# VectorE's and ScalarE's order in the first 21 steps taken from a list schedule that the program works out while it is made

## Chip, cores and metric

The kernel runs on one core of a Trainium2 chip. The metric is the time of one execution on the device in microseconds (us). Before the change the median of three runs is 1159.02 us (1157.17 to 1159.98). The engines are TensorE (PE in the rows: matrix products; PEld is its loading of weights), VectorE (DVE), ScalarE (ACT), GpSimd (POOL) and SyncE (SP, which here issues the DMA transfers). Each engine works through its own instructions in the order in which the program was written. "Granted clock" is the share of full speed that TensorE was given; it has two levels, 2.4 GHz (1.0) and 1.2 GHz (0.5).

## What is computed

A decaying linear attention (32 heads, 768 tokens, width 64) gives 3072 tokens of width 512. Two feed-forward layers follow, each 512 to 2048 to 512, the first with a leaky ReLU between its products, the second with an ELU. The weights come in as float64.

```python
def _moe_ref(x, w_in, w_out):
    h = x @ w_in
    g = np.maximum(0.01 * h, h)
    return (g @ w_out).astype(np.float32)

def _moe2_ref(x, w_in, w_out):
    h = x @ w_in
    g = np.where(h > 0.0, h, np.exp(np.minimum(h, 0.0)) - 1.0)
    return (g @ w_out).astype(np.float32)

x = attention(q, k, v)            # 4 x 8 x 768 x 64 -> 3072 x 512
return _moe2_ref(_moe_ref(x, w_in1, w_out1), w_in2, w_out2)
```

## The kernel before

**Tiling.** The tokens are cut into 6 blocks of 512 (`j`), the hidden width of 2048 into 16 slices of 128 (`m`). One *step* is one slice for one block: a first product (`gemm1`, L254: 12 matmuls of 128x512 into `h`), the leaky ReLU on ScalarE (`leaky`, L343, tile `gf`), a split of the result into a high and a low part (high: a cast on ScalarE, tile `ghi`; low: a subtraction on VectorE, tile `glo`; for steps 4 to 7 both lie in a waiting tile, `gx`), and a second product (`gemm2`, L273: 12 matmuls that add up in two accumulators `y0` and `y1`). Every product is made of three matmuls, high by high, high by low and low by high, so that a result near float32 comes out.

**Weights.** The float64 weights of a slice are turned into a high and a low float32 part on the chip. This *conversion* is done piece by piece. A piece is half a slice for slices 0 to 3 (8 pieces: the half of the first product and that of the second) and a whole slice for slices 4 to 15 (12 pieces). Its operations are `c_put` (ScalarE, L113), `c_exp` (VectorE, two instructions, L116 and L117), a bias (ScalarE, L120), `c_top` (VectorE, L123), `c_low` (VectorE, L127), `c_sign` (VectorE, L131), `c_mul` (VectorE, L134, with a cast on ScalarE, L172) and `c_split` (VectorE, L176). `conv_ops` (L182) puts them into one queue, and `conv(n)` (L198) takes n of the VectorE operations from its front.

**Order of the first layer.** The first layer's steps are numbered by visits: steps 0 to 3 are block 0 with slices 0 to 3, steps 4 to 11 block 1 with slices 0 to 7, steps 12 to 23 block 0 with slices 4 to 15, steps 24 to 31 block 1 with slices 8 to 15. Then come blocks 2 to 5 with all 16. A table `plan` (L505, L506) says in which order the first products run (0, 4, 1, 5, 2, 6, 3, 7, 8, 9, ...), up to which step the second products have to be done behind each (`drain`, L299), and how many operations of the conversion are put in at two places of each step (`conv(n1)` between the first product and its leaky ReLU, `conv(n2)` at the step's end). `need` (L211) forces the conversion of a piece that a product is about to read. When the last slice of a part visit is done (steps 3 and 11), `drain` copies the accumulators out (tile `ysb`, two copies on VectorE, two on ScalarE, L320) and SP writes them to HBM; the next block's second product can't begin before that.

**Around it.** Before the first step, the eight attention chunks of blocks 0 and 1 run. Chunk 8 and later are worked between the steps from step 23 on; the loads of chunks 8 and 9 are issued at steps 8 and 9. The weights of slices 6 to 15 are loaded by `load_w` at the ends of steps, into tiles that other data (chunks, waiting tiles, `ysb`) held before. The order on VectorE, ScalarE and SP is that in which this loop is written.

Of the kernel before, what the change touches and what calls it, by code (L numbers as in the profile page):

```python
# [20 lines left out]
F32 = mybir.dt.float32  # L21
F32R = mybir.dt.float32r
# [5 lines left out]
ALU = mybir.AluOpType  # L28
# [4 lines left out]
P = 128  # L33
# [5 lines left out]
BLK = 512  # L39
CPB = BLK // C  # L40
NB = NT // BLK
KD = DM // P
MF = DFF // P
HM = MF // 2
V0 = 4
# [9 lines left out]
def body(ctx: ExitStack, tc: tile.TileContext, kkv, w1, w2, tabs, out):  # L55
    nc = tc.nc
    big = ctx.enter_context(tc.tile_pool(name="big", bufs=1))
    wp = ctx.enter_context(tc.tile_pool(name="wp", bufs=1))
    cv = ctx.enter_context(tc.tile_pool(name="cv", bufs=2))
    gp = ctx.enter_context(tc.tile_pool(name="gp", bufs=2))  # L60
    ps = ctx.enter_context(tc.tile_pool(name="ps", bufs=1, space=PSUM))
# [3 lines left out]
    pscr = [dp.tile([P, KD, BLK], F32, name=f"pscr{j}") for j in range(2)]  # L65
# [6 lines left out]


    W = 2 * BLK
    raw, wt, cvt, exps, ready = {}, {}, {}, [], {}
    nload = nload2 = 0


# [1 line left out]
    pieces = [(m, a, 1) for m, a in halves] + [(m, 0, 2) for m in range(V0, MF)]  # L80
    loaded = set()
# [37 lines left out]
    def bias(e):  # L119
        nc.scalar.activation(e.bitcast(I16), e, AF.Relu, bias=ebias, scale=2.0**3)  # L120
# [22 lines left out]
    def c_exp(i):  # L143
        e = cvt[i][0]
        s = cv.tile([P, i[2] * BLK], U16, tag="s", name="s", bufs=1)
        cvt[i].append(s)
        masks(e, s)
        exps.append(e)

    def c_top(i):  # L150
        m, a, n = i
# [10 lines left out]
    def c_mul(i):  # L162
        e, _, f = cvt.pop(i)
        power(e, f)
        m, a, n = i
        t = place(m, a, n, F32R, "w")
        for k in range(n):
            wt[0, m, a + k] = t[:, k * W : (k + 1) * W]
        t = t.rearrange("p (a b c) -> p a b c", a=n, b=2)
        f = f.rearrange("p (a c) -> p a c", a=n)  # L170
        ready[i] = t, f
        nc.scalar.copy(t[:, :, 0, :], f)  # L172

    def c_split(i):
# [7 lines left out]
    def conv_ops():  # L182
        yield c_put, pieces[0]
        for n, i in enumerate(pieces):
            yield c_exp, i
            if n:
# [6 lines left out]
            yield c_mul, i  # L193
        yield c_split, pieces[-1]

    queue = list(conv_ops())

    def conv(n):  # L198

        while queue and queue[0][1][:2] in loaded:  # L200
            op, i = queue[0]
            if op is not c_put:
                if not n:
                    break
                n -= 1
            queue.pop(0)
            op(i)
            while exps:
                bias(exps.pop(0))

    def need(m, a):  # L211
        while (m, a) not in split_done:
            conv(1)
# [129 lines left out]
    def leaky(h):  # L343
        gf = gp.tile([P, BLK], F32, tag="gf", name="gf", bufs=2)
        nc.scalar.activation(gf, h, AF.Prelu, alpha=0.01)  # L345
        return gf


    with ExitStack() as actx:
        ab = actx.enter_context(tc.tile_pool(name="ab", bufs=1))  # L350
        ap_ = actx.enter_context(tc.tile_pool(name="ap", bufs=2))
        aps = actx.enter_context(tc.tile_pool(name="aps", bufs=1, space=PSUM))
# [102 lines left out]
        nload = V0  # L455
# [20 lines left out]
        o = outputs(0, *next(banks))  # L476
# [6 lines left out]
        for c in range(1, 2 * CPB):  # L483
# [3 lines left out]
            o = outputs(c, *next(banks))  # L487
# [20 lines left out]
        for n, (s, upto, n1, n2) in enumerate(plan):  # L508
# [11 lines left out]
            if 4 <= s < 8:  # L520
                i = 2 * (s % 2)
                ghi, glo = g[s] = [wait[s // 2 - 2][:, i + k, :] for k in range(2)]
                nc.scalar.copy(ghi, gf)
                nc.vector.tensor_tensor(glo, gf, ghi.bitcast(F32), ALU.subtract)
            else:
                split_g(s, gf, nc.vector, gp, 3)
            drain(upto, stage_w if vi < 2 or m < m0 + 2 and vi == 2 else stage_f)
            c = sc_at.get(s)
            if c is not None:
                sc = scores(c, aps, "x")  # L530
                prep(c)
                masked(c, sc, ap_, "pt")
            conv(n2)
            if s in (8, 9):
                att_load(2 * CPB + s - 8)
            if nload < (MF - 1 if s > 11 else MF - 3) or vi > 1 and m > m0 + 1:
                load_w()
            if vi > 3:

                if m == 2 and npre < 2 * MF:  # L540
                    pre_load()
                if 2 < m < MF - 1:
                    pre(m < MF - 2)
            if m0 > 0 and m == m1 - 3:
                need(MF - 1, 1)
                reload(0, j, stage_f)


    with ExitStack() as ectx:
# [44 lines left out]
        for s in range(NA, 2 * NS):  # L594
            ph, j, m, (_, _, m0, m1, vi) = steps[s]
            if s % 4 == 0:
                h = ps.tile([P, BLK], F32, tag="h", name="h")
# [3 lines left out]
            if ph == 0:  # L601
                gf = leaky(h)
# [80 lines left out]
```

## Time and profile before

| | us |
|---|---|
| median of three runs | 1159.02 (1157.17 to 1159.98) |
| the profiled execution, its own time | 1159.4 |
| its span, from the first to the last instruction | 1157.6 |
| TensorE busy | 1138.3 |
| VectorE busy | 653.2 |
| ScalarE busy | 542.2 |
| mean granted clock of TensorE | 0.995 |

The 1.8 us between the profiled execution's time and its span lie outside the instructions. All times inside the trace count from the start of the span. A row of a timeline gives the start, the length and the operation, and in brackets how long the engine was idle before it and who ended the wait. A busy TensorE isn't TensorE at its full clock, so the granted clock is read beside the busy time.

### The profile page before, as it was taken

The page shows a single profiled execution, that of the slowest core. Times are in us where ns is not written, and L with a number is a line of the kernel's source. Part 1 is how long each engine was busy: PE and PEld are TensorE (multiplying, and loading weights), DVE is VectorE, ACT ScalarE, POOL GpSimd, SP SyncE. Part 2 cuts the span into 40 slices and gives each one's busy share as a digit, 9 for nine tenths or more (in the row PEclk, how much of TensorE's full clock was granted, in tenths as well). Part 3 has the DMA queues.
Part 4 walks back from the last instruction along what each step waited for, and adds up shares of the span by engine and source line. Part 5 has one row for each costly group of instructions (what it writes and reads, how often), then busy time and mean ns, then how long its engine had stood idle before and what let it go on. Part 6 is the DMA issues. An engine that isn't in the chain of part 4 may idle for free.

```text
span 1157.6 us, 14906 instructions
## 1 busy us (share of the span) xinstructions
PE 1138.3 (98%) x6024; PEld 930.9 (80%) x6024; DVE 653.2 (56%) x1049; ACT 542.2 (47%) x901; POOL 93.2 (8%) x77
## 2 busy tenths in 40 slices
PE   8989999999999999999999999999999999999998
PEld 6767788788888888888888888888888888888886
DVE  5879773235654564651212666666666666766655
ACT  2555552224444443441323654654654655555553
POOL 4000001102221222220000000000000000000000
PEclk9989999999999999999999999999999999999999
DMA  9931303334554554430645400100100100000000
GB/s 377 377 129 54 109 21 116 115 115 154 193 200 154 193 195 151 161 131 1 218 183 196 148 19 1 55 19 1 55 19 1 55 19 1 37 1 1 37 1 37
DMA packets 29877, 117.10 MB, mean 101 GB/s; under 512 B 3312, under 2 KB 3312, under 8 KB 23792
## 3 DMA queue, kind: packets, MB, share of 16 engines
q1 hardware_dynamic: 29808, 116.15, 27.4%
q8 instruction: 47, 0.77, 0.3%
q14 instruction: 22, 0.18, 0.1%
HBM read 84.68 MB, written 31.46 MB: 100 GB/s over the span
## 4 chain that ended last, share of the span: by engine, by line
PE 89%; DVE 4%; ACT 2%; issue 0%; ACTq 0%; DVEq 0%
PE y L286 43%; PE h L263 42%; PE sc L393 2%; PE o L411 1%; DVE f L134 1%; DVE f L127 1%; PE o L419 1%; ACT w L172 1%; PE o L415 1%; ACT e L120 0%; DVE glo L270 0%; DVE e L131 0%; DVE f L123 0%; DVE w L176 0%; ACT gf L345 0%; ACT ghi L269 0%
## 5 line engine op out<-in xcount | busy, mean ns | idle before, releaser
L263 PE MATMUL h<-xhi,w 128*128 128x512 f32 x1536 | 506.2, 391 | 1.8 <-DVE w L176 1.2
L270 DVE TENSOR_TENSOR glo<-gf,ghi 128x512 fp32r<-128x512 f32 x188 | 131.0, 697 | 375.6 <-ACT ghi L269 373.6
L263 PEld LDWEIGHTS h<-xhi,w 128*128 128x128 f32 x1536 | 288.0, 188 | 65.6 <-DVE w L176 2.5
L263 PE MATMUL h<-xlo,w 128*128 128x512 f32 x768 | 299.0, 389 | 0.0
L286 PE MATMUL y<-ghi,w 128*128 128x512 f32 x736 | 247.3, 398 | 5.7 <-DVE w L176 2.4
L286 PE MATMUL y<-w,ghi 128*128 128x512 f32 x768 | 236.5, 389 | 0.0
L286 PEld LDWEIGHTS y<-ghi,w 128*128 128x128 f32 x736 | 140.1, 191 | 38.6 <-DVE w L176 2.9
L286 PEld LDWEIGHTS y<-w,ghi 128*128 128x128 f32 x768 | 144.1, 188 | 29.9
L263 PEld LDWEIGHTS h<-xlo,w 128*128 128x128 f32 x768 | 144.3, 188 | 29.5
L572 ACT ACTIVATE n<-h 128x512 f32<-128x512 f32 x96 | 57.4, 598 | 224.3 <-PE h L263 224.3
L286 PE MATMUL y<-w,glo 128*128 128x512 f32 x384 | 149.4, 389 | 0.0
L286 PE MATMUL y<-glo,w 128*128 128x512 f32 x368 | 144.7, 393 | 0.0
L345 ACT ACTIVATE gf<-h 128x512 f32<-128x512 f32 x96 | 56.9, 593 | 164.4 <-PE h L263 164.1
L269 ACT CAST ghi<-gf 128x512 fp32r<-128x512 f32 x188 | 115.3, 613 | 5.8 <-DVE gf L583 3.4
L286 PEld LDWEIGHTS y<-w,glo 128*128 128x128 f32 x384 | 72.1, 188 | 15.0
L286 PEld LDWEIGHTS y<-glo,w 128*128 128x128 f32 x368 | 70.3, 191 | 14.4
L580 DVE SCALAR_TENSOR_TENSOR a<-n,a 128x512 f32<-128x512 f32 x96 | 65.6, 684 | 5.9 <-ACT n L575 5.9
L582 DVE SCALAR_TENSOR_TENSOR t<-a,t 128x512 f32<-128x512 f32 x96 | 66.4, 692 | 3.3
L583 DVE SCALAR_TENSOR_TENSOR gf<-h,t 128x512 f32<-128x512 f32 x96 | 66.4, 691 | 3.3
L120 ACT ACTIVATE e<-e,ebias 128x512 int16<-128x512 uint16 (+1 forms) x52 | 42.7, 821 | 50.9 <-DVE e L117 50.9
L581 DVE SCALAR_TENSOR_TENSOR t<-n,t 128x512 f32<-128x512 f32 x96 | 65.7, 685 | 0.0
L573 ACT ACTIVATE t<-n 128x512 f32<-128x512 f32 x96 | 60.7, 632 | 3.1
(51 smaller groups left out, 806.3 us busy)
## 6 DMA issues: line engine op xcount, KB each, us to landing
kv<-in_kkv SPq DMA_DIRECT2D x23, 1024.0 KB, 6.2
raw<-in_w SPq DMA_DIRECT2D x40, 512.0 KB, 3.8
wscr<-raw SPq DMA_DIRECT2D x32, 512.0 KB, 2.6
raw<-in_w SPq DMA_DIRECT2D x12, 1024.0 KB, 11.5
w<-wscr SPq DMA_DIRECT2D x12, 1024.0 KB, 4.7
xs<-yscr SPq DMA_DIRECT2D x12, 512.0 KB, 3.7
out<-osb SPq DMA_DIRECT2D x24, 256.0 KB, 2.9
yscr<-ysb SPq DMA_DIRECT2D x16, 256.0 KB, 2.8
```

The source lines that it names most:

```text
L120: nc.scalar.activation(e.bitcast(I16), e, AF.Relu, bias=ebias, scale=2.0**3)
L263: nc.tensor.matmul(h, a, x, start=(n == 0), stop=(n == 3 * KD - 1))
L269: nc.scalar.copy(ghi, gf)
L270: eng.tensor_tensor(glo, gf, ghi.bitcast(F32), ALU.subtract)
L286: nc.tensor.matmul(acc[d], lhsT, rhs, start=(first and n == 0), stop=(last and n == 2))
L345: nc.scalar.activation(gf, h, AF.Prelu, alpha=0.01)
L572: nc.scalar.activation(n, h, AF.Relu, scale=-1.0)
L573: nc.scalar.activation(t, n, AF.Tanh, scale=-0.5)
L580: nc.vector.scalar_tensor_tensor(out=a, in0=n, scalar=1.0, in1=a, op0=ALU.add, op1=ALU.mult)
L581: nc.vector.scalar_tensor_tensor(out=t, in0=n, scalar=1.0, in1=t, op0=ALU.add, op1=ALU.mult)
L582: nc.vector.scalar_tensor_tensor(out=t, in0=a, scalar=2.0, in1=t, op0=ALU.add, op1=ALU.mult)
L583: nc.vector.scalar_tensor_tensor(out=gf, in0=h, scalar=0.0, in1=t, op0=ALU.max, op1=ALU.add)
```

## The change

The first 21 entries of `plan` no longer run in a loop with counts for the conversion. A new function `scheduled` lists every operation of these entries as a task with its engine (P, A, V, Q for TensorE, ScalarE, VectorE, SP), a cost in us and the tasks that it waits for. TensorE's order stays as it was. Each task gets a latest beginning, worked back from when TensorE would want its result if it never waited; then a list schedule goes forward in time from zero on all engines and lets each engine take, among the tasks that are able to begin first, the one with the smallest latest beginning. The program is written in the order that comes out. The bias and the cast of a piece, which were issued together with `c_exp` and `c_mul`, are tasks of their own (`c_bias`, `c_cast`). Each accumulator is copied out by one instruction (`leave`), `y0` on VectorE and `y1` on ScalarE, and written by one DMA of 512 KB where there were two of 256 KB. The loads of slices 6 to 15 are tasks too, and the loads of chunks 8 and 9 come after the 21 entries.

```diff
-            if op is not c_put:
+            if op not in (c_put, c_bias, c_cast):
...
-        plan = [(0, -1, 2, 2), (4, -1, 2, 2), (1, 0, 4, 3), (5, 0, 2, 2), (2, 1, 4, 3), (6, 1, 2, 2), (3, 3, 2, 3), (7, 5, 3, 5)]
-        plan += [(s, s - 2, 3 if s < 12 else 2, 3 if s == 8 else 2) for s in range(8, NA)]
+        plan = [(0, -1), (4, -1), (1, 0), (5, 0), (2, 1), (6, 1), (3, 3), (7, 5)]
+        plan += [(s, s - 2) for s in range(8, NA)]
+        NL = 21
...
+        def scheduled(plan):
+            ops = {c_put: ("A", 0.58, 1.07), c_exp: ("V", 0.65, 0.85), c_bias: ("A", 0.63, 1.08), c_top: ("V", 0.42, 0.72),
+                   c_low: ("V", 0.6, 1.22), c_sign: ("V", 0.4, 0.7), c_mul: ("V", 0.6, 1.22), c_cast: ("A", 0.55, 1.05),
+                   c_split: ("V", 0.6, 1.22)}
...
+            def leave(s, i):
...
+                t = ends[s][:, 2 * i : 2 * i + 2, :]
+                (nc.scalar.copy if i else nc.vector.tensor_copy)(t, acc[i])
+                nc.sync.dma_start(out=part[0, j][:, 2 * i : 2 * i + 2, :], in_=t)
...
+                task(("g1", s), "P", 2.72, [half_split(m, 0), ("leaky", old) if n > 1 else None], lambda n=n, s=s: first_product(n, s))
+                pe.append(("g1", s))
+                task(("leaky", s), "A", 0.62, [("g1", s)] + ([("ghi", old), ("glo", old)] if n > 1 else []), lambda s=s: leak(s))
...
+                        deps = [("ghi", at), ("glo", at), half_split(m, 1)]
+                        if m == m0 and left_by is not None:
+                            deps.append(("leave", left_by, i))
+                        task(("g2", at, i), "P", 1.36, deps, lambda at=at, i=i: second(at, i))
...
+            latest, t = {}, 0.0
+            for x in pe:
+                latest[x] = t
+                t += tasks[x][1]
...
+            def begin(x):
+                if x not in latest:
+                    latest[x] = min([begin(y) for y in after[x]], default=t) - tasks[x][1] - 0.2
+                return latest[x]
+
+            free = dict.fromkeys("PAVQ", 0.0)
...
+            while able:
+                pick = {}
+                for x, r in able.items():
+                    eng = tasks[x][0]
+                    if eng == "P" and x != pe[0]:
+                        continue
+                    c = (max(r, free[eng]), begin(x))
+                    if eng not in pick or c < pick[eng][0]:
+                        pick[eng] = c, x
+                (now, _), x = min(pick.values(), key=lambda v: v[0])
...
+                fn()
...
+        scheduled(plan[:NL])
+        for c in range(2 * CPB, 2 * CPB + 2):
+            att_load(c)
+        for n, (s, upto) in enumerate(plan[NL:], NL):
...
-            conv(n1)
...
-            conv(n2)
-            if s in (8, 9):
-                att_load(2 * CPB + s - 8)
-            if nload < (MF - 1 if s > 11 else MF - 3) or vi > 1 and m > m0 + 1:
-                load_w()
```

Three places show what moves. In the rows a line number of the changed kernel differs from that of the kernel before (L177 is L172, L181 is L176, L350 is L345, L590 and L593 are the high and the low part of every step, L572 is L320).

The first is ScalarE right behind the attention, from the first `c_put` of the steps on. Before:

```order
L113 COPY e<-raw 128x512
L345 ACTIVATE gf<-h 128x512
L269 CAST ghi<-gf 128x512
L172 CAST w<-f 128x512
L120 ACTIVATE e<-e,ebias 128x512
```

and after:

```order
L113 COPY e<-raw 128x512
L177 CAST w<-f 128x512
L113 COPY e<-raw 128x512
L350 ACTIVATE gf<-h 128x512
L590 CAST ghi<-gf 128x512
L120 ACTIVATE e<-e,ebias 128x512
```

Step 0's leaky ReLU (`gf<-h`) now stands behind the cast of a piece (`w<-f`) and the next piece's `c_put`.

The second is VectorE around the second products of steps 2 and 3. The last one-half pieces end there, the first whole slice begins. Before (the first `w` is the piece that step 2's second product reads, the second that of step 3, the `glo` is step 3's):

```order
L116 TENSOR_SCALAR s<-e 128x512
L117 TENSOR_SCALAR e<-e 128x512
L524 TENSOR_TENSOR gx<-gf,gx 128x512
L176 TENSOR_TENSOR w<-f,w 128x512
L123 TENSOR_SCALAR f<-raw 128x512
L127 SCALAR_TENSOR_TENSOR f<-f,raw 128x512
L131 TENSOR_TENSOR e<-e,s 128x512
L270 TENSOR_TENSOR glo<-gf,ghi 128x512
L134 SCALAR_TENSOR_TENSOR f<-f,e 128x512
L116 TENSOR_SCALAR s<-e 128x1024
L117 TENSOR_SCALAR e<-e 128x1024
L176 TENSOR_TENSOR w<-f,w 128x512
```

and after (the same two pieces; the first `glo` is step 2's, the last step 3's):

```order
L181 TENSOR_TENSOR w<-f,w 128x512
L593 TENSOR_TENSOR glo<-gf,ghi 128x512
L131 TENSOR_TENSOR e<-e,s 128x512
L134 SCALAR_TENSOR_TENSOR f<-f,e 128x512
L116 TENSOR_SCALAR s<-e 128x1024
L117 TENSOR_SCALAR e<-e 128x1024
L123 TENSOR_SCALAR f<-raw 128x1024
L181 TENSOR_TENSOR w<-f,w 128x512
L593 TENSOR_TENSOR gx<-gf,gx 128x512
L127 SCALAR_TENSOR_TENSOR f<-f,raw 128x1024
L131 TENSOR_TENSOR e<-e,s 128x1024
L134 SCALAR_TENSOR_TENSOR f<-f,e 128x1024
```

Step 3's `glo` is the row right behind these twelve. The split of the piece for step 2 no longer stands behind the low part of step 6 (`gx`), and step 3's low part stands behind three more operations of slice 4 (128x1024).

The third is VectorE where block 1's first half ends (step 11) and `y0` is copied out. Before (the first `glo` is step 12's, the second step 13's):

```order
L270 TENSOR_TENSOR glo<-gf,ghi 128x512
L116 TENSOR_SCALAR s<-e 128x1024
L117 TENSOR_SCALAR e<-e 128x1024
L176 TENSOR_TENSOR w<-f,w 128x2x512
L123 TENSOR_SCALAR f<-raw 128x1024
L127 SCALAR_TENSOR_TENSOR f<-f,raw 128x1024
L270 TENSOR_TENSOR glo<-gf,ghi 128x512
L320 COPY ysb<-y_821 128x512 x2
L131 TENSOR_TENSOR e<-e,s 128x1024
```

and after:

```order
L593 TENSOR_TENSOR glo<-gf,ghi 128x512
L116 TENSOR_SCALAR s<-e 128x1024
L117 TENSOR_SCALAR e<-e 128x1024
L123 TENSOR_SCALAR f<-raw 128x1024
L134 SCALAR_TENSOR_TENSOR f<-f,e 128x1024
L127 SCALAR_TENSOR_TENSOR f<-f,raw 128x1024
L572 COPY ysb<-y_819 128x1024
L593 TENSOR_TENSOR glo<-gf,ghi 128x512
```

The copy of `y0` (`ysb<-y`) now stands ahead of step 13's low part.

## Rows read from the trace of the kernel before

**Rows 1.** The page's first part: busy us of each engine (share of the span).

```profile
PE 1138.3 (98%) x6024; PEld 930.9 (80%) x6024; DVE 653.2 (56%) x1049; ACT 542.2 (47%) x901; POOL 93.2 (8%) x77
```

**Rows 2.** Windows by stage: stretch, then busy us per engine, PEclk, DMA share, GB/s.

```profile
0.00:38.00 38.00, 30.48 (x464) 23.21 (x468) 25.75 (x41) 9.77 (x15) 16.76 (x18) 1.00 0.96 388
38.00:76.00 38.00, 34.08 (x148) 26.90 (x141) 27.64 (x58) 20.90 (x34) 0.00 (x0) 0.91 0.45 187
76.00:130.00 54.00, 50.33 (x209) 39.60 (x208) 46.16 (x60) 33.23 (x42) 1.46 (x1) 0.97 0.37 128
130.00:162.00 32.00, 32.00 (x143) 26.49 (x142) 25.46 (x34) 17.57 (x22) 0.00 (x0) 1.00 0.13 48
```

**Rows 3.** Timeline of TensorE: first matmuls of products (start us, us, operation).

```profile
38.33 0.50 PE L263 MATMUL h<-xhi,w 128*128 128x512 f32 x1
...
108.87 0.39 PE L263 MATMUL h<-xhi,w 128*128 128x512 f32 x1
...
114.31 0.39 PE L263 MATMUL h<-xhi,w 128*128 128x512 f32 x1
...
129.22 0.40 PE L263 MATMUL h<-xhi,w 128*128 128x512 f32 x1
```

**Rows 4.** Timeline of TensorE: matmuls that waited, and step 7's first product.

```profile
36.24 1.09 PE L411 MATMUL o<-pt,kv 128*64 128x128 f32 x16 [1.59 <-DVE pt L399]
...
64.89 0.50 PE L286 MATMUL y<-ghi,w 128*128 128x512 f32 x1 [1.14 <-ACT w L172]
...
68.05 1.22 PE L286 MATMUL y<-ghi,w 128*128 128x512 f32 x2 [2.42 <-DVE w L176]
...
76.02 0.39 PE L263 MATMUL h<-xhi,w 128*128 128x512 f32 x1
...
124.81 0.47 PE L286 MATMUL y<-ghi,w 128*128 128x512 f32 x1 [2.18 <-DVE ysb L320]
```

**Rows 5.** Windows of half a us where the granted clock changes (columns as in rows 2).

```profile
74.00:74.50 0.50, 0.50 (x3) 0.38 (x3) 0.00 (x0) 0.00 (x0) 0.00 (x0) 0.86 0.00 0
...
125.00:125.50 0.50, 0.50 (x3) 0.42 (x3) 0.47 (x2) 0.00 (x0) 0.00 (x0) 0.84 1.09 426
...
128.50:129.00 0.50, 0.50 (x4) 0.36 (x3) 0.36 (x1) 0.50 (x2) 0.00 (x0) 0.74 0.88 270
```

**Rows 6.** Timeline of VectorE, the same columns.

```profile
41.57 0.69 DVE L127 SCALAR_TENSOR_TENSOR f<-f,raw 128x512 f32<-128x512 uint32 x1
...
61.98 0.42 DVE L123 TENSOR_SCALAR f<-raw 128x512 uint32<-128x512 uint32 x1
...
64.43 0.29 DVE L117 TENSOR_SCALAR e<-e 128x512 uint16<-128x512 uint16 x1
66.70 0.69 DVE L524 TENSOR_TENSOR gx<-gf,gx 128x512 fp32r<-128x512 f32 x1 [1.98 <-ACT gx L523]
67.30 0.69 DVE L176 TENSOR_TENSOR w<-f,w 128x512 fp32r<-128x512 f32 x1
...
76.04 0.68 DVE L123 TENSOR_SCALAR f<-raw 128x1024 uint32<-128x1024 uint32 x1
...
80.21 0.43 DVE L117 TENSOR_SCALAR e<-e 128x1024 uint16<-128x1024 uint16 x1
...
123.38 1.28 DVE L320 COPY ysb<-y 128x512 f32<-128x512 f32 x2
```

**Rows 7.** Timeline of ScalarE, the same columns.

```profile
39.71 0.65 ACT L113 COPY e<-raw 128x512 int16<-128x512 int16 x1
...
43.99 0.62 ACT L172 CAST w<-f 128x512 fp32r<-128x512 f32 x1 [1.36 <-DVE f L134]
...
65.38 0.58 ACT L345 ACTIVATE gf<-h 128x512 f32<-128x512 f32 x1
```

**Rows 8.** Timeline of GpSimd: the first operation behind chunk 8's scores (PE sc).

```profile
179.56 1.30 POOL L380 TENSOR_TENSOR kv<-kv,tab 128x512 f32<-128x512 f32 x1 [91.09 <-PE sc L393]
```

**Rows 9.** The page's last part, chunk loads: count, KB each, median us to landing.

```profile
kv<-in_kkv SPq DMA_DIRECT2D x23, 1024.0 KB, 6.2
```

More of the change, by code (lines that the diff above doesn't have):

```diff
@@ L147, in c_exp, with c_bias @@
         masks(e, s)
-        exps.append(e)
+    def c_bias(i):
+        bias(cvt[i][0])
     def c_top(i):
@@ L171, in c_mul, with c_cast @@
         ready[i] = t, f
+    def c_cast(i):
+        t, f = ready[i]
         nc.scalar.copy(t[:, :, 0, :], f)
@@ L185, in conv_ops @@
             yield c_exp, i
+            yield c_bias, i
             if n:
@@ new lines, in scheduled, with task, key, second @@
+        def scheduled(plan):
+            nonlocal acc, done, npart
+            tasks, pe = {}, []
+            def task(key, eng, cost, deps, fn):
+                tasks[key] = eng, cost, [d for d in deps if d is not None], fn
+            ops = {c_put: ("A", 0.58, 1.07), c_exp: ("V", 0.65, 0.85), c_bias: ("A", 0.63, 1.08), c_top: ("V", 0.42, 0.72),
+                   c_low: ("V", 0.6, 1.22), c_sign: ("V", 0.4, 0.7), c_mul: ("V", 0.6, 1.22), c_cast: ("A", 0.55, 1.05),
+                   c_split: ("V", 0.6, 1.22)}
+            left = set(queue)
+            chain = {c_put: (), c_exp: ((c_put, 0), (c_sign, 1)), c_bias: ((c_exp, 0),), c_top: ((c_exp, 0), (c_split, 2)),
+                     c_low: ((c_top, 0),), c_sign: ((c_bias, 0), (c_low, 0)), c_mul: ((c_sign, 0),), c_cast: ((c_mul, 0),),
+                     c_split: ((c_cast, 0),)}
+            def key(op, i):
+                return (op.__name__, i) if (op, i) in left else None
+            for n, i in enumerate(pieces):
+                for op, (eng, one, two) in ops.items():
+                    if (op, i) not in left:
+                        continue
+                    deps = [key(o, pieces[n - k]) for o, k in chain[op] if n >= k]
+                    if n:
+                        deps.append(key(op, pieces[n - 1]))
+                    if op is c_put:
+                        deps += [key(c_mul, pieces[n - 2]) if n > 1 else None, ("load", i[0]) if i[:2] not in loaded else None]
+                    task(key(op, i), eng, one if i[2] == 1 else two, deps, lambda op=op, i=i: op(i))
+            queue.clear()
+            seconds = {}
+            ends = {}
+            def second(s, i):
+                ph, j, m, (_, _, m0, m1, _) = steps[s]
+                if m == m0:
+                    acc[i] = ps.tile([P, 2, BLK], F32, tag=f"y{i}", name=f"y{i}")
+                ghi, glo = g[s]
+                w = wt[0, m, 1]
+                for d in (2 * i, 2 * i + 1):
+                    ds = slice(d * P, (d + 1) * P)
+                    for n, (lhsT, rhs) in enumerate(((w[:, ds], ghi), (w[:, ds], glo), (w[:, BLK + d * P : BLK + (d + 1) * P], ghi))):
+                        nc.tensor.matmul(acc[i][:, d % 2], lhsT, rhs, start=(m == m0 and n == 0), stop=(m == m1 - 1 and n == 2))
+            def leave(s, i):
+                nonlocal npart
+                j = steps[s][1]
+                if i == 0:
+                    part[0, j] = pscr[npart]
+                    npart += 1
+                    ends[s] = wp.tile([P, 4, BLK], F32, tag=f"w{MF - 1}", name="ysb")
+                t = ends[s][:, 2 * i : 2 * i + 2, :]
+                (nc.scalar.copy if i else nc.vector.tensor_copy)(t, acc[i])
+                nc.sync.dma_start(out=part[0, j][:, 2 * i : 2 * i + 2, :], in_=t)
+            acc = [None, None]
+            at, left_by = -1, None
+            own = [s for s, _ in plan if s not in later]
+            users = {}
+            def first_product(n, s):
+                h = (aps if n % 2 else ps).tile([P, BLK], F32, tag="z" if n % 2 else "h", name="h")
+                users[s] = h
+                gemm1(0, steps[s][2], steps[s][1] % 2, h)
+            def leak(s):
+                users[s] = leaky(users[s])
+            def high(s):
+                g[s] = later[s] if s in later else [gp.tile([P, BLK], F32R, tag=x, name=x, bufs=3) for x in ("ghi", "glo")]
+                nc.scalar.copy(g[s][0], users[s])
+            def glow(s):
+                nc.vector.tensor_tensor(g[s][1], users.pop(s), g[s][0].bitcast(F32), ALU.subtract)
+            def half_split(m, a):
+                i = (m, a, 1) if m < V0 else (m, 0, 2)
+                return key(c_split, i)
+            for n, (s, upto) in enumerate(plan):
+                m = steps[s][2]
+                old = plan[n - 2][0] if n > 1 else None
+                prev = plan[n - 1][0] if n else None
+                task(("g1", s), "P", 2.72, [half_split(m, 0), ("leaky", old) if n > 1 else None], lambda n=n, s=s: first_product(n, s))
+                pe.append(("g1", s))
+                task(("leaky", s), "A", 0.62, [("g1", s)] + ([("ghi", old), ("glo", old)] if n > 1 else []), lambda s=s: leak(s))
+                deps = [("leaky", s)]
+                if n:
+                    deps += [("ghi", prev)]
+                if s not in later:
+                    k = own.index(s)
+                    if k > 2:
+                        deps.append(("g2", own[k - 3], 1))
+                task(("ghi", s), "A", 0.53, deps, lambda s=s: high(s))
+                task(("glo", s), "V", 0.6, [("ghi", s)] + ([("glo", prev)] if n else []), lambda s=s: glow(s))
+                while at < upto:
+                    at += 1
+                    _, j, m, (_, _, m0, m1, _) = steps[at]
+                    for i in range(2):
+                        deps = [("ghi", at), ("glo", at), half_split(m, 1)]
+                        if m == m0 and left_by is not None:
+                            deps.append(("leave", left_by, i))
+                        task(("g2", at, i), "P", 1.36, deps, lambda at=at, i=i: second(at, i))
+                        pe.append(("g2", at, i))
+                    if m == m1 - 1:
+                        for i in range(2):
+                            task(("leave", at, i), "A" if i else "V", 1.1 if i else 1.25,
+                                 [("g2", at, i), ("leave", at, 0) if i else None], lambda at=at, i=i: leave(at, i))
+                        left_by = at
+            done = at
+            for k, m in enumerate(range(nload, MF)):
+                deps = [("load", m - 1)] if k else []
+                deps += {MF - 1: [("leave", x, 1) for x in (V0 - 1, V0 + HM - 1)], MF - 2: [("g2", x, 1) for x in (4, 5)],
+                         MF - 3: [("g2", x, 1) for x in (6, 7)]}.get(m, [])
+                task(("load", m), "Q", 2.6, deps, load_w)
+            latest, t = {}, 0.0
+            for x in pe:
+                latest[x] = t
+                t += tasks[x][1]
+            after = {x: [] for x in tasks}
+            for x, (_, _, deps, _) in tasks.items():
+                for d in deps:
+                    after[d].append(x)
+            def begin(x):
[3 more added lines that the diff above has]
+            free = dict.fromkeys("PAVQ", 0.0)
+            over = {}
+            open_ = {x: len(tasks[x][2]) for x in tasks}
+            able = {x: 0.0 for x in tasks if not open_[x]}
+            order = []
+            while able:
[3 more added lines that the diff above has]
+                    if eng == "P" and x != pe[0]:
+                        continue
+                    c = (max(r, free[eng]), begin(x))
+                    if eng not in pick or c < pick[eng][0]:
+                        pick[eng] = c, x
+                (now, _), x = min(pick.values(), key=lambda v: v[0])
+                del able[x]
+                eng, cost, _, fn = tasks[x]
+                if eng == "P":
+                    pe.pop(0)
+                free[eng] = now + cost
+                over[x] = now + cost + (2.2 if eng == "Q" else 0.0)
+                order.append(x)
+                fn()
+                for y in after[x]:
+                    open_[y] -= 1
+                    if not open_[y]:
+                        able[y] = max(over[d] + (0.2 if tasks[d][0] != tasks[y][0] else 0.0) for d in tasks[y][2])
+            assert len(order) == len(tasks)
+            acc = [acc[d // 2][:, d % 2] for d in range(4)]
@@ L519, in body @@
                     att_load(c + 2)
[L520 to L527, printed above, removed]
+            split_g(s, gf, nc.vector, gp, 3)
+            drain(upto, stage_f)
             c = sc_at.get(s)
```

8 lines of the change are left out of this document (3 added, 5 removed).

## The prediction

> **What bounds the kernel now.** I read the page first: TensorE is busy 98% of the span [rows 1], so time can only be won where TensorE idles or runs at half clock. The windows by stage show where that is [rows 2]. From 130 to 162 us TensorE is busy all the time at granted clock 1.00; from 38 to 130 us it is idle for 3.9 + 3.7 us and the clock averages 0.91 and 0.97. That stretch is the one which the change orders anew. VectorE is busy 73% and 85% of it (27.6 of 38, 46.2 of 54): loaded, but with room.
>
> How much TensorE loses there comes from its timeline. At full clock one first and one second product take 5.44 us (108.87 to 114.31 [rows 3]), so a product 2.72. The first matmul starts at 38.33, and a matmul behind a pause is about 0.1 longer, so count from 38.44. At 129.22 the first product of step 15 begins, and 28 products lie before it (15 first, 13 second). At full pace it would begin at 38.44 + 28 x 2.72 = 114.6. TensorE has **lost 14.6 us** by then, and loses nothing more up to 162. That is all that this change can win.
>
> What the loss consists of: up to step 7's first product, with 11 products before it, 76.02 - (38.44 + 11 x 2.72) = 7.7 us, the rest, 6.9, later. The waits named [rows 4]: step 2's second product waits 1.14 for ScalarE's cast and 2.42 for VectorE's split of its piece, and step 12's waits 2.18 for the copy of `y0`. Behind both the clock was at 1.2 GHz: until 74.1 the first time (matmuls from 68.05 on, so (74.1 - 68.05)/2 = 3.0 us lost), and from 125.2 to 128.7 the second (1.7 us lost) [rows 4, 5]. The rest are waits under 0.6 us for splits.
>
> Why they were late is the order. The split at 67.30 stands behind step 6's low part, which waited 1.98 us for ScalarE's high part, and ScalarE had come to step 6's leaky ReLU only at 65.38 [rows 6, 7]. The copy of `y0` at 123.38 stands behind step 13's low part in the same way. Neither engine was short of time; work that was urgent stood behind work that wasn't able to begin.
>
> **The change, part by part.**
>
> *TensorE's work* is the same, in the same order: nothing.
>
> *The conversion's order.* I lay out VectorE's new order from the same start as before (up to `c_top` of the third piece the rows agree, so `c_low` begins at 41.57 [rows 6]). Prices: a whole one-half piece without its split goes from 61.98 to 64.43 plus 0.2 for its last instruction, 2.66 us; a split or a low part follows its predecessor by 0.60 (66.70 to 67.30); the same six instructions of a whole slice take 80.21 + 0.34 - 76.04 = 4.5 [rows 6].
>
> First wait. ScalarE issues the cast of the third piece and the next `c_put` ahead of step 0's leaky ReLU. VectorE's `c_low`, `c_sign`, `c_mul` (0.61 + 0.45 + 0.69) end at 43.3, the cast (0.62, the next instruction 0.54 after its start) and the `c_put` (0.65) let the leaky ReLU begin at about 44.4 and end at 45.0 [rows 6, 7]. Step 1's first product needs that tile of `h` free and would come at 38.44 + 2 x 2.72 = 43.9: **1.2 us of waiting** that wasn't there. Ends: nothing, if ScalarE gets the leaky ReLU in earlier; 1.7, if nothing of these instructions overlaps.
>
> Second wait. Before step 3's low part VectorE now has 1.67 (the rest of the third piece), five one-half pieces at 2.66, six splits and six low parts at 0.61, and six instructions of slice 4 at 4.5: 26.8 us. It begins at 68.4 and ends at 69.1. TensorE wants it, ten products and the first wait after 38.44, at 66.8; one matmul (0.23) needs the high part alone. **2.1 us of waiting.** Ends: 0.2, if all the 51 instructions overlap as splits do, and 4, if none does. VectorE has no idle time in this stretch, so this wait is a matter of work done too early: the three operations of slice 4 ahead of it (some 3 us) aren't urgent. The list was made for engines that are all free at zero; VectorE comes 3.2 us late from the attention.
>
> After that I find no wait. Slices 5 to 7 cost VectorE some 5.6 us each, one per step of 5.44, but they start early: with the rest of slice 4, the copy of `y0` and two low parts it has 3 x 5.6 + 1.1 + 1.2 + 1.2 = 20.3 us from 69.1 on, so slice 7's split ends at about 90. Step 11's first product, 20 products and both waits after 38.44, comes at 96. Cover 6 us. Slices 8 to 15 are wanted a slice per step only from step 16 on and are made from step 9 on. The 7 us of waits before splits and the copy go.
>
> *The copies of the accumulators.* One instruction of 1024 for two that took 1.28 together [rows 6]: the same. It can begin once `y0`'s half is done and has a whole first product (2.72 us) and half a second product as cover; nothing on the path. Without the cover it would cost its 1.3 us.
>
> *Loads.* Those of slices 13 to 15 wait for the same tiles as before. Slice 15's needs step 11's `ysb` written out; it comes some 11 us earlier with it, as its `c_put` does. The loads of chunks 8 and 9 now queue behind that one on SP. VectorE's copy for step 11 ended at 124.7 [rows 6] and ends about 11 us earlier now, so with the write and slice 15's load I allow until 125. Chunk 8's scores stood just before 179.56 [rows 8], so about 168 now; a chunk lands in 6.2 us [rows 9]. Cover over 30 us, cost nothing; once it is gone, us for us.
>
> **The sum.** 14.6 lost before, less 1.2, 2.1 and some 0.3 for the slower first matmul behind each of three pauses: 11.0 us won. The profiled execution took 1159.4, so 1148.4. It stands 0.4 above the median of the runs (1159.02), so **1148.0**.
>
> **The rivals.**
>
> *The clock falls behind the second wait.* The clock fell behind a pause of 2.18 and behind one of 1.14 and 2.42 with two matmuls between; it stayed up, by the windows, through the attention's 1.59 at 36.24 [rows 2, 4, 5]. The new pause, about 0.9 and 1.2 with one matmul between, lies between these, nearer to the one that fell in sum, broken up as it is. Price 1.7 us as the second time (3.0 as the first): 1149.7. The Trainium skill (TensorE: Matmul & The Clock Gate, Part 1: The HAM clock gate) says that the clock is halved after TensorE has been idle and given back after sustained activity, and that the monitor runs free of the kernel, so the same pause may fall on either side; the rows agree with the first and can't show the second.
>
> *Engines in step.* If VectorE is quicker than I lay it out (its lower end) and ScalarE comes early, both waits shrink to nearly nothing: 1159.0 - 14.6 = 1144.4. Against it: VectorE's 26.8 us are counted from rows of the same instructions.
>
> *The early part isn't won.* If the 3.2 us that VectorE comes late upset the order more than I see (each engine in turn behind the other), the first 76 us lose what they lost before, 7.7, and only the later 6.9 are won: 1152.1.
>
> *Slower.* The first wait could come back with every step: a leaky ReLU behind a cast that waits for VectorE, and the product after next behind it. At 1.2 in each of the 21 steps it is 25 us against 14.6: 1169. The point from which it decides is 0.7 us per step. Against it speak two things: a product waits for the leaky ReLU of two before, which leaves up to 5 us of play where step 0 had 2.7, and VectorE is ahead from step 8 on.
>
> *It doesn't do what it says*: the rows at the three places show that the order did change, so this has no share.
>
> **How the numbers follow.** Forecast as summed: 0.55. Clock falls: 0.23. Early part isn't won: 0.11. Engines in step: 0.06. Slower: 0.02. Something unseen that leaves it within 0.3% (3.5 us, about what a measurement of this kernel can tell from no change): 0.03. Faster by more than 0.3% is the sum of the first four, 0.95; within, 0.03; slower, 0.02. The range goes from the case without waits, 1144.4, to just under the early part not won, 1152.0; it leaves out 0.16.
>
> **What would show it.** In the changed kernel's timeline of TensorE: a wait of about 1.2 for ScalarE's leaky ReLU at 43.9, one of about 2 for VectorE's low part at 67, and none for splits or `ysb` after; step 15's first product at about 118 in place of 129.22; VectorE without idle time from 41 to 69; chunk 8's first GpSimd operation some 11 us earlier. It is wrong if waits for splits of slices 5 to 7 remain, if the clock is below 1.0 in a window behind 70, or if step 15's product comes later than 122.

## The result and the profile after

The changed kernel takes 1148.54 us (median of four runs, 1148.27 to 1148.82); the kernel before took 1158.30 in the same comparison (1157.17 to 1159.98). The ratio is 0.9915, with a 95% interval of 0.9897 to 0.9932. The profiled execution took 1148.57, its span 1146.8 in place of 1157.6.

| | before | after |
|---|---|---|
| median, us | 1158.30 | 1148.54 |
| span of the profiled execution | 1157.6 | 1146.8 |
| first matmul of step 0 | 38.33 | 38.61 |
| first product of step 7 begins | 76.02 | 71.90 |
| first product of step 15 begins | 129.22 | 118.14 |
| lost to TensorE by step 7 / by step 15 | 7.7 / 14.6 | 3.3 / 3.3 |

The last line is counted as in the prediction: start of step 0's first matmul, plus 0.11, plus 11 or 28 products at 2.72, taken from the start of the product. The same count is used for every experiment below.

The page's first part of the kernel after, which answers [rows 1], and the same windows by stage as in [rows 2] (busy us of PE, PEld, DVE, ACT, POOL, then granted clock, DMA share, GB/s):

```profile
PE 1132.1 (99%) x6024; PEld 928.2 (81%) x6024; DVE 650.8 (57%) x1047; ACT 542.7 (47%) x899; POOL 92.7 (8%) x77
```

```profile
38.00:76.00 38.00, 35.65 (x171) 28.55 (x168) 36.31 (x69) 26.75 (x42) 0.00 (x0) 1.00 0.57 240
76.00:130.00 54.00, 54.00 (x240) 44.72 (x239) 51.37 (x69) 36.76 (x45) 1.28 (x1) 1.00 0.30 119
130.00:162.00 32.00, 32.00 (x143) 26.50 (x142) 16.40 (x20) 13.64 (x18) 0.00 (x0) 1.00 0.10 33
```

In the first stretch TensorE idles 2.35 us where it idled 3.92, in the second not at all, and the clock is 1.00 in both. VectorE is busy 36.3 of 38 us where it was 27.6: it does the same work earlier, and between 130 and 162 it has 16.4 us to do where it had 25.5.

The timeline of TensorE after (start us, length, operation, and in brackets the idle time before and who ended it), all its waits from step 0 to step 15, with the first matmuls of the products of steps 7 and 15, answers [rows 3, 4]:

```profile
45.42 0.50 PE L268 MATMUL h<-xhi,w 128*128 128x512 f32 x1 [1.07 <-ACT gf L350]
...
68.17 0.51 PE L562 MATMUL y<-ghi,w 128*128 128x512 f32 x1 [0.67 <-ACT ghi L590]
69.28 0.50 PE L562 MATMUL y<-glo,w 128*128 128x512 f32 x1 [0.61 <-DVE glo L593]
...
71.90 0.39 PE L268 MATMUL h<-xhi,w 128*128 128x512 f32 x1
...
118.14 0.39 PE L268 MATMUL h<-xhi,w 128*128 128x512 f32 x1
```

Two waits are left, and the new order makes both: for step 0's leaky ReLU (`gf`), and, in two parts around one matmul, for step 3's high part (`ghi`) and low part (`glo`). No wait for a split or for a copy of an accumulator is left.

The two engines at these places. ScalarE first (step 0's leaky ReLU, then step 3's), then VectorE (its one wait between 41 and 69, the three operations of slice 4 ahead of step 3's low part, and the copy of step 11's `y0`). They answer [rows 6, 7]:

```profile
43.70 0.62 ACT L177 CAST w<-f 128x512 fp32r<-128x512 f32 x1 [3.05 <-DVE f L134]
44.22 0.65 ACT L113 COPY e<-raw 128x512 int16<-128x512 int16 x1
44.78 0.59 ACT L350 ACTIVATE gf<-h 128x512 f32<-128x512 f32 x1
...
65.84 1.13 ACT L113 COPY e<-raw 128x1024 int16<-128x1024 int16 x1
66.84 0.62 ACT L350 ACTIVATE gf<-h 128x512 f32<-128x512 f32 x1
```

```profile
46.05 0.69 DVE L593 TENSOR_TENSOR glo<-gf,ghi 128x512 fp32r<-128x512 f32 x1 [0.37 <-ACT ghi L590]
...
65.54 1.22 DVE L127 SCALAR_TENSOR_TENSOR f<-f,raw 128x1024 f32<-128x1024 uint32 x1
66.68 0.68 DVE L131 TENSOR_TENSOR e<-e,s 128x1024 uint16<-128x1024 uint16 x1
67.39 1.22 DVE L134 SCALAR_TENSOR_TENSOR f<-f,e 128x1024 f32<-128x1024 f32 x1
68.54 0.68 DVE L593 TENSOR_TENSOR glo<-gf,ghi 128x512 fp32r<-128x512 f32 x1
...
111.54 1.23 DVE L572 COPY ysb<-y 128x1024 f32<-128x1024 f32 x1 [0.72 <-PE y L562]
```

The copy of `y0` now waits for TensorE and not TensorE for the copy. On ScalarE step 3's leaky ReLU stands behind a `c_put` of slice 5 (1.13 us) that nobody needs yet; I had not counted that one.

### The profile page after: what moved, and what is told of

It reads as the page before. It is cut to its first block, busy times and chain, and to the rows that moved or that the text cites. A ratio compares the mean times of both kernels' runs of the same rounds, so it can differ in the third digit from the quotient of the medians.

```text
span 1146.8 us, 14900 instructions
## 1 busy us (share of the span) xinstructions
PE 1132.1 (99%) x6024; PEld 928.2 (81%) x6024; DVE 650.8 (57%) x1047; ACT 542.7 (47%) x899; POOL 92.7 (8%) x77
## 4 chain that ended last, share of the span: by engine, by line
PE 94%; DVE 4%; DMA 1%; ACT 0%; issue 0%; SPq 0%; ACTq 0%
PE h L268 44%; PE y L291 41%; PE y L562 4%; PE sc L398 2%; PE o L416 2%; DMA kv<-in_kkv 1%; PE o L424 1%; PE o L420 1%; DVE f L127 1%; DVE pt L404 0%; DVE f L134 0%; DVE xlo L441 0%; DVE e L131 0%; DVE w L181 0%; DVE s L116 0%; DVE f L123 0%
## 5 line engine op out<-in xcount | busy, mean ns | idle before, releaser
L275 DVE TENSOR_TENSOR glo<-gf,ghi 128x512 fp32r<-128x512 f32 x171 | 119.3, 698 | 370.5 <-ACT ghi L274 370.5
L291 PE MATMUL y<-ghi,w 128*128 128x512 f32 x616 | 204.3, 393 | 0.0
L350 ACT ACTIVATE gf<-h 128x512 f32<-128x512 f32 x96 | 57.2, 596 | 186.7 <-PE h L268 186.3
L291 PEld LDWEIGHTS y<-ghi,w 128*128 128x128 f32 x616 | 115.6, 188 | 26.4 <-issue 2.4
L291 PE MATMUL y<-glo,w 128*128 128x512 f32 x308 | 119.9, 389 | 0.0
L274 ACT CAST ghi<-gf 128x512 fp32r<-128x512 f32 x171 | 104.7, 612 | 5.3 <-DVE gf L747 3.4
L291 PEld LDWEIGHTS y<-glo,w 128*128 128x128 f32 x308 | 57.8, 188 | 11.6
```

Of the source, the lines that this page charges most:

```text
L291: nc.tensor.matmul(acc[d], lhsT, rhs, start=(first and n == 0), stop=(last and n == 2))
```

## Experiments

Ratios are to the kernel before on the same chip and in the same rounds.

**1. The old order in the new frame.** Everything else of the change stays; the list schedule's order is replaced by the order of the kernel before, written with the same tasks (`taken` is filled by the old counts per step).

```diff
-                (now, _), x = min(pick.values(), key=lambda v: v[0])
...
+            counts = [(2, 2), (2, 2), (4, 3), (2, 2), (4, 3), (2, 2), (2, 3), (3, 5)]
+            counts += [(3 if s < 12 else 2, 3 if s == 8 else 2) for s, _ in plan[8:]]
...
+            order = taken
+            for x in order:
+                tasks[x][3]()
```

> The changed kernel with VectorE's and ScalarE's operations of all 21 entries put back into the relative order of the kernel before; the single copy per accumulator, its one write, the tasks for the loads and the later loads of chunks 8 and 9 stay as changed. Theory (the order alone makes the gain): as before, 1158.3 within 1.5 us, with step 2's second product waiting some 3.5 us in two parts and step 12's some 2, and the clock at 1.2 GHz behind both. Rival (the copies and the loads carry a part): 1155 or less, with step 12's wait shorter than 1.5 us.

Measured: 1158.64 us, ratio 0.9988 (0.9977 to 1.0000), as before. The single copies, the larger writes, the tasks for the loads and the later chunk loads are together worth 0 to 0.23% (up to 2.7 us); the order makes the gain. TensorE's timeline shows the old waits, the first two to the hundredth of [rows 4], the third 0.06 shorter, and between them two for splits of slices 6 and 7:

```profile
64.63 0.50 PE L563 MATMUL y<-ghi,w 128*128 128x512 f32 x1 [1.14 <-ACT w L177]
...
67.78 1.22 PE L563 MATMUL y<-ghi,w 128*128 128x512 f32 x2 [2.42 <-DVE w L181]
...
94.94 0.73 PE L268 MATMUL h<-xhi,w 128*128 128x512 f32 x2 [0.53 <-DVE w L181]
...
101.61 0.73 PE L268 MATMUL h<-xhi,w 128*128 128x512 f32 x2 [0.53 <-DVE w L181]
...
122.61 0.47 PE L563 MATMUL y<-ghi,w 128*128 128x512 f32 x1 [2.12 <-DVE ysb L573]
```

The profiled execution is the fastest of its ten (1155.89; the slowest took 1160.02), and its windows tell why. The clock was back at 1.00 by 71 (before: 74.1), and behind the 2.12 at 122.61 it didn't fall at all. In half a us each, the fall and the return (columns as in rows 2):

```profile
67.00:67.50 0.50, 0.00 (x0) 0.00 (x0) 0.50 (x2) 0.50 (x2) 0.00 (x0) 1.00 0.06 16
67.50:68.00 0.50, 0.22 (x1) 0.22 (x2) 0.50 (x2) 0.47 (x2) 0.00 (x0) 0.51 0.00 0
...
70.50:71.00 0.50, 0.50 (x3) 0.40 (x2) 0.47 (x2) 0.48 (x1) 0.00 (x0) 0.58 0.00 0
71.00:71.50 0.50, 0.50 (x4) 0.41 (x3) 0.50 (x2) 0.33 (x1) 0.00 (x0) 1.00 0.00 0
```

**2 and 3. One half of the change each.** In the first the old order runs through step 7's entry, to just before step 8's first product, and the list schedule goes on from there (`cut` is that place in the old order `taken`); in the second the list schedule runs up to the same product, and the rest stands in the old relative order.

```diff
+                if len(order) < cut:
+                    x = taken[len(order)]
+                    now = max(able[x], free[tasks[x][0]])
```

```diff
+            order = order[: order.index(("g1", 8))]
+            order += [x for x in taken if x not in order]
```

> The old order up to step 7's entry, the list schedule (going on from there) behind it. If the losses of the early and the late part stand apart as the prediction has them (7.7 and 6.9 us): 1148.5 + 7.7 - 3.3 = 1152.9. Rival (VectorE is still late from the early part, so that splits of slices 5 and 6 are awaited): some 1 us more, 1153.9, with waits for splits between 80 and 105 us. Step 12's wait for the copy of y0 is gone by either.

> The list schedule up to step 7's entry, the old relative order of the rest behind it. If the two losses stand apart: 1148.5 + 6.9 = 1155.4, with waits for splits at steps 9 to 11 and for the copy at step 12. Rival (the late waits were the early lateness handed on, since the old late order starts with VectorE ahead here): only the copy of y0 is awaited, 1.4 us: 1149.9, or 1151.6 if the clock falls behind it.

Measured: 1154.54 us, ratio 0.9959 (0.9940 to 0.9978), for the old early part, and 1150.52, ratio 0.9921 (0.9900 to 0.9943), for the old late part. The rival holds in both: the two losses don't stand apart. For 3 the times show it (1155.4 lies far off); for 2 they can't tell 1152.9 from 1153.9, and the waits for splits decide it. By the same count of lost time:

| | lost by step 7 | from step 7 to step 15 |
|---|---|---|
| before | 7.7 | 6.9 |
| old order, both parts (1) | 6.3 | 4.9 |
| old early, list late (2) | 7.3 | 1.6 |
| list early, old late (3) | 3.3 | 1.6 |
| changed kernel | 3.3 | 0.0 |

Either half of the change takes 3 to 5 us out of the late loss. So most of it was lateness handed on. In 1, by the starts of the products, the splits of slices 5 to 7 cost 2.4 us and the copy of `y0` another 2.4; the same late order that starts with VectorE ahead (3) waits once in this part, for the copy, and loses 1.6. A list that starts with VectorE late (2) still waits for splits of slices 5 and 6 (0.2 and 1.4 us):

```profile
117.34 0.47 PE L563 MATMUL y<-ghi,w 128*128 128x512 f32 x1 [1.32 <-DVE ysb L573]
```

```profile
96.81 0.72 PE L268 MATMUL h<-xhi,w 128*128 128x512 f32 x2 [1.04 <-DVE w L181]
```

(the first row is TensorE's in 3, the second in 2.) VectorE's rows in 2 show what stands in front of that split: the `c_low` of slice 7, which nobody needs yet. The cast that the split reads had ended at 94.17.

```profile
94.39 1.23 DVE L127 SCALAR_TENSOR_TENSOR f<-f,raw 128x1024 f32<-128x1024 uint32 x1
95.53 1.22 DVE L181 TENSOR_TENSOR w<-f,w 128x1024 fp32r<-128x1024 f32 x1
```

**4. The list told of the true start.** One line:

```diff
-            free = dict.fromkeys("PAVQ", 0.0)
+            free = dict(P=0.0, A=1.27, V=3.1, Q=0.0)
```

> One line of the changed kernel: the list schedule begins with VectorE free at 3.1 us and ScalarE at 1.27 us after TensorE's first product, as the trace of before shows, where all engines began at zero. Theory (the two waits left come from the list's wrong start): both waits gone, step 1's first product follows without a pause and step 3's second product waits under 0.3 us: 1148.5 - 3.2 = 1145.3. Rival (VectorE's 26.8 us of work before step 3's low part are the bound, whatever the order): the second wait stays at 1.5 us or more: 1147 to 1148.5.

Measured: 1145.42 us (1145.27 to 1147.55), ratio 0.9878 (0.9860 to 0.9896). TensorE waits for nothing from step 0 to step 15; its windows and the first product of step 15:

```profile
38.00:76.00 38.00, 38.00 (x183) 31.28 (x182) 36.62 (x70) 27.67 (x42) 0.00 (x0) 1.00 0.58 243
76.00:130.00 54.00, 54.00 (x240) 44.72 (x239) 51.09 (x68) 37.60 (x46) 1.07 (x1) 1.00 0.30 117
```

```profile
114.92 0.39 PE L268 MATMUL h<-xhi,w 128*128 128x512 f32 x1
```

At full pace step 15's first product would begin at 38.55 + 0.11 + 28 x 2.72 = 114.82: 0.1 us lost. The order that came out leaves ScalarE's leaky ReLU of step 0 in front of the cast, and VectorE's low part of step 3 in front of the three operations of slice 4, which now follow it:

```profile
41.63 0.60 ACT L350 ACTIVATE gf<-h 128x512 f32<-128x512 f32 x1 [1.03 <-PE h L268]
42.26 0.63 ACT L590 CAST ghi<-gf 128x512 fp32r<-128x512 f32 x1
43.59 0.62 ACT L177 CAST w<-f 128x512 fp32r<-128x512 f32 x1 [0.70 <-DVE f L134]
```

```profile
65.27 0.69 DVE L593 TENSOR_TENSOR glo<-gf,ghi 128x512 fp32r<-128x512 f32 x1
65.87 1.22 DVE L127 SCALAR_TENSOR_TENSOR f<-f,raw 128x1024 f32<-128x1024 uint32 x1
67.00 0.69 DVE L131 TENSOR_TENSOR e<-e,s 128x1024 uint16<-128x1024 uint16 x1
```

VectorE's work ahead of step 3's low part was not the bound; the order of it was.

**5. Half the lateness.** The same line with V=1.5 and A=0.

> The list begins with VectorE free at 1.5 us (half its lateness), all else at zero. The two waits should come apart: step 1's first product waits no longer, step 3's second product still waits about 1.3 us for its low part: 1145.4 + 1.4 = 1146.8. Rival (one lateness, one effect): both waits halved, 1147.

Measured: 1146.98 us (1146.50 to 1147.16), ratio 0.9891 (0.9874 to 0.9908). The two waits come apart as the theory has it: the first is gone, of the second one part is left, and 1.6 us are lost by step 15:

```profile
67.66 0.50 PE L562 MATMUL y<-glo,w 128*128 128x512 f32 x1 [0.85 <-DVE glo L593]
```

**6 and 7. The second wait made longer.** Step 3's low part is computed three and five times over.

```diff
             def glow(s):
+                for _ in range(2 if s == 3 else 0):
+                    nc.vector.tensor_tensor(g[s][1], users[s], g[s][0].bitcast(F32), ALU.subtract)
```

> The changed kernel with step 3's low part subtracted three times over (two repeats of 0.60 us on VectorE, the same result). Theory (this wait is on the path, us for us): TensorE waits for it 1.2 us longer, 1149.7. Clock rival: behind a pause of 0.9 and 2.1 us with one matmul between, the clock falls in at least some executions, as it does behind 1.4 and 2.6 before, which adds 1 to 3 us to those: up to 1152.7, and runs that spread over 2 us or more.

> The same with four repeats, 2.4 us. Theory: us for us, 1150.9. Clock rival: the clock falls in most executions, 1152 to 1154. A third way: VectorE's lateness is handed on to the splits of slices 5 to 7, whose cover is about 5 us: no waits there by the theory.

Measured: 1152.77 us (1151.30 to 1153.74), ratio 0.9940 (0.9921 to 0.9960), with two repeats, and 1153.99 (1152.36 to 1156.22), ratio 0.9952 (0.9936 to 0.9967), with four. The repeats cost VectorE more than the 0.60 each that the expectations reckon with: the two of 6 hold the low part back from 70.69 to 72.14, 1.45 us, and the four of 7 from 67.78 to 70.67, 2.89 us, 0.72 each:

```profile
70.69 1.41 DVE L594 TENSOR_TENSOR glo<-gf,ghi 128x512 fp32r<-128x512 f32 x2
```

```profile
67.78 2.86 DVE L594 TENSOR_TENSOR glo<-gf,ghi 128x512 fp32r<-128x512 f32 x4
```

TensorE's wait for the low part, 0.61 in the changed kernel, grows by 1.48 and 2.91: us for us. Time lost by step 15 is 6.3 and 8.6 us where the changed kernel loses 3.3: 3.0 and 5.3 more. The rest is the clock. TensorE's two matmuls of the longer pauses (6, then 7), and the clock's windows of 6:

```profile
72.88 0.79 PE L562 MATMUL y<-glo,w 128*128 128x512 f32 x1 [2.09 <-DVE glo L595]
```

```profile
71.42 0.79 PE L562 MATMUL y<-glo,w 128*128 128x512 f32 x1 [3.52 <-DVE glo L595]
```

```profile
72.50:73.00 0.50, 0.12 (x1) 0.12 (x1) 0.50 (x2) 0.36 (x1) 0.00 (x0) 0.77 0.00 0
73.00:73.50 0.50, 0.50 (x2) 0.40 (x3) 0.47 (x2) 0.00 (x0) 0.00 (x0) 0.50 0.00 0
...
76.00:76.50 0.50, 0.50 (x3) 0.42 (x2) 0.50 (x1) 0.00 (x0) 0.00 (x0) 0.81 0.00 0
```

In 6 the matmuls from 72.9 to 76.2 run at 1.2 GHz, which loses (76.2 - 72.9) / 2 = 1.6 us: with the 1.45 that is the 3.0, to a tenth. In 7 the matmuls from 71.4 to 76.6 do, which loses 2.6: with the 2.9 that is the 5.3, to two tenths. (The pauses of before that the first expectation gives as 1.4 and 2.6 are 1.14 and 2.42 in [rows 4].) No wait for a split follows in either, so the cover of slices 5 to 7 holds against 2.9 us. The medians aren't split up like this: the profiled execution of 6 (1153.74) lies 5.2 us above that of the changed kernel, and 2.1 of these come from step 0, which began at 40.75 in place of 38.61 (last section).

**8. Four copies.** Each emptying in four copies and four writes, as before, at the places that the list gives.

```diff
-                t = ends[s][:, 2 * i : 2 * i + 2, :]
-                (nc.scalar.copy if i else nc.vector.tensor_copy)(t, acc[i])
-                nc.sync.dma_start(out=part[0, j][:, 2 * i : 2 * i + 2, :], in_=t)
+                for d in range(2):
+                    t = ends[s][:, 2 * i + d, :]
+                    (nc.scalar.copy if i else nc.vector.tensor_copy)(t, acc[i][:, d])
+                    nc.sync.dma_start(out=part[0, j][:, 2 * i + d, :], in_=t)
```

> The changed kernel with four copies and four writes of 256 KB per emptying, as before, at the places that the list gives them. Theory (worth nothing): 1148.5 within 0.5 us. Rival (one copy and one write save a part): 0.5 to 2 us more.

Measured: 1148.27 us (1147.63 to 1150.40), ratio 0.9901 (0.9880 to 0.9921): no difference to the changed kernel. Lost by step 15: 3.3 us, the same.

**9. Side by side.** The changed kernel and the list with the true start (4) on one chip, in the same rounds.

> The changed kernel itself, on the same chip and in the same rounds as the next, so that the two are compared directly. By the traces it should stay 3.2 us behind the list with the true start: ratio to before 0.991 to 0.992.

> The list that begins with VectorE free at 3.1 us and ScalarE at 1.27 us, beside the changed kernel. Theory: 3.2 us less than the changed kernel (the two waits and the slower matmuls behind them). Rival (the difference of the two earlier sessions was the chip's): within 1 us of it.

Measured: 1149.61 us (1148.58 to 1150.89), ratio 0.9921 (0.9906 to 0.9936), and 1146.42 (1145.32 to 1148.58), ratio 0.9894 (0.9877 to 0.9912). The medians are 3.2 us apart; the count of lost time in their own profiled executions gives 2.9 (3.27 against 0.40; in the second step 3's low part came some 0.2 us late, which it didn't in experiment 4). The intervals of the two ratios overlap (0.9906 to 0.9912), and the runs just meet: the fastest of the first and the slowest of the second took 1148.58. Both kernels spread because executions differ at their start (last section).

## Why the prediction was right, and where it wasn't

Forecast 1148.0 in 1144.4 to 1152.0, measured 1148.54. That the two lie so close is in part luck with the base. The forecast gain is 11.0; the profiled executions give 10.8, but the medians of the comparison 9.8. The forecast took what the profiled execution of before lost for what every execution loses, while the four runs of before took 1157.17 to 1159.98. By its steps:

- **What bounds, and what is to be won.** 14.6 us lost by step 15's first product was all that the change could win. Experiment 4 wins all but 0.1 of it, and its span is 14.0 below that of before (1143.6 against 1157.6; step 0 began 0.2 later). Right.
- **The first wait.** Forecast 1.2 for step 0's leaky ReLU, with step 1's first product due at 43.9; measured, it was due at 44.16 (38.61 + 0.11 + 2 x 2.72) and began at 45.42, 1.26 late, behind the cast and the `c_put` named. Experiments 4 and 5 show that it hangs on the list's start.
- **The second wait.** Forecast 2.1 for VectorE's low part, in two parts of about 0.9 and 1.2; measured 0.67 and 0.61, with the slower matmuls 1.8 in all ((71.90 - 67.34) - 2.72, where 67.34 is when step 3's second product could begin). VectorE's count came out right to 0.1: from its `c_low` at 41.85 to the low part at 68.54 are 26.7 us, forecast 26.8. But 0.37 of them are a wait for step 0's high part at 46.05, where the prediction had VectorE without idle time, so the work itself was counted some 0.5 too high. The wait came out shorter because, each against the start of the steps (which had moved by 0.28), VectorE came 0.14 earlier than forecast and TensorE 0.2 later. The cause, unurgent work of slice 4 put ahead because the list began with all engines free, is shown by 4 and 5. The part of ScalarE in it (the `c_put` of slice 5 at 65.84) was missed: it set the first of the two pieces.
- **The sum.** Lost after the change: forecast 3.6, measured 3.3. Won by step 15: forecast 11.0, measured 14.6 - 3.3 = 11.3. Step 15's product: forecast about 118, measured 118.14.
- **Costs at nothing.** The copies: shown by 8. The loads: chunk 8's first GpSimd operation behind its scores began at 168.45, 11.1 us earlier than [rows 8], with the chunk's load issued at 117.36; the frame as a whole is worth 0 to 0.23% by 1.
- **The clock.** The pause stayed harmless in all four runs of the changed kernel (mean clock 0.999 to 1.000) and cost 1.6 us in the profiled execution of experiment 6, where it is 1.5 us longer. The price was right, and 1.5 us more of waiting made the rival come true there. The same kernel's six runs in 9 have mean clocks of 0.998 to 1.000 and take up to 1150.89; the profiled one lost 3.3 us at full clock as before, and whether the clock of the slowest fell behind this pause or in the attention isn't known.

What was wrong is a step of a rival: "The early part isn't won", with "only the later 6.9 are won: 1152.1". It took the two losses to stand apart. Experiment 2 is that case and gives 1154.54, outside the stated range; experiment 3 gives 1150.52 where the same reasoning had 1155.4. Of the late loss 1.6 us were the late order's own when VectorE comes in time, another 3.3 came from the early lateness (1: 4.9, less the 1.6 of 3), and in the profiled execution of before 1.7 from the clock. The forecast itself didn't use that step, since both parts change.

What stays open: how much of the 1.6 us of experiment 2 is lateness handed on. Its split of slice 6 stands behind slice 7's `c_low` (94.39), and without it could have begun 1.1 us sooner. So most of that loss looks like the same fault as the second wait, unurgent work put ahead by a list that doesn't know how late the engines are; no run tried it.

## What to carry to other kernels

Count an engine's lost time from the starts of its own pieces of work at full pace, and read from the order who stands in front of the one that is awaited: an engine that is 73% busy can still be the cause, since urgent work waits behind work that was written first. A list schedule made in the program is only as good as the state it starts from: 3.1 us of lateness that it wasn't told of cost 3.2 us of TensorE's time, and one line with the measured start took them away. Losses in a row of stages need not add up, as experiments 2 and 3 show; undo each half by itself before you credit a stage.

## What the runs showed of the hardware

The clock's answer to nearly the same pause differs from execution to execution. Behind 2.18 us at 124.81 it fell before [rows 4, 5], behind 2.12 us at 122.61 in experiment 1 it didn't; behind the same 1.14 and 2.42 it came back at 74.1 in one and at 71 in the other. The runs of a kernel with such pauses spread: 1155.89 to 1160.02 in experiment 1, against 1148.27 to 1148.82 and, in 9, 1148.58 to 1150.89 for the changed kernel. The Trainium skill (TensorE: Matmul & The Clock Gate, Part 1: The HAM clock gate) says that the monitor runs free of the kernel. The different answers fit that; no run here shows the monitor itself.

Executions also differ in the attention, before the steps, and that moves them as a whole. In the profiled execution of the list with the true start, side by side (9), step 0 began at 41.48, where it began at 38.55 in experiment 4. TensorE first waited 2.71 us for a chunk's load, where its longest wait for one in experiment 4 was 0.57, and later 2.01 for VectorE; behind both waits the clock fell. Why the load came late stays open. TensorE's two rows, then the windows, with the clock below 1.00 in three of four stretches:

```profile
19.38 1.16 PE L398 MATMUL sc<-kv 64*128 64x128 f32 x16 [2.71 <-DMA kv<-in_kkv]
...
33.73 1.60 PE L416 MATMUL o<-pt,kv 128*64 128x128 f32 x16 [2.01 <-DVE pt L404]
```

```profile
20.00:25.00 5.00, 5.00 (x72) 4.58 (x71) 2.80 (x5) 0.72 (x2) 3.33 (x3) 0.66 1.01 424
25.00:30.00 5.00, 5.00 (x106) 4.38 (x102) 5.00 (x9) 1.64 (x3) 2.71 (x2) 1.00 1.01 414
30.00:35.00 5.00, 2.99 (x50) 2.56 (x48) 4.96 (x7) 1.19 (x2) 2.39 (x3) 0.92 1.03 420
35.00:40.00 5.00, 5.00 (x80) 4.29 (x77) 4.99 (x8) 1.55 (x3) 1.28 (x1) 0.74 1.04 434
```

In 6 and 8, where step 0 began at 40.75 and 40.72, the clock fell at a wait for a load of 1.82 and 1.91 us that ended near 8 us; at one of 1.61 (the changed kernel in 9) and 1.66 (5) in the same place it stayed at 1.00. I had taken such differences for noise of a few tenths; over the profiled executions step 0's start differs by up to 3.7 us (37.83 in 7, 41.48 in 9), more than the last step of improvement here, and only a count from step 0's own start takes them out.
